# RWKV-5 attention and a multiplicative FFN in one kernel: the general arm's loads and stores move from SyncE's queue to ScalarE's

## The chip, the cores and the metric

The kernel runs on 1 core of one Trainium2 chip. Its time is the device time of one execution in microseconds (us). The time before is the median of three runs; one more execution was recorded by the hardware profiler, and the profile is of that one.

The core has five engines with an instruction stream each: TensorE (PE in the profile; its weight loads are PEld), VectorE (DVE), ScalarE (ACT), GpSimd (POOL) and SyncE (SP). SyncE computes nothing: it issues DMAs and waits on semaphores. ScalarE can issue DMAs too, between its own computations.

## The reference

Two blocks follow each other. The first is a linear attention with a decaying state, for 4 batches, 8 heads, 768 steps and a head size of 48:

```python
def _attn_ref(r, k, v, w, u):
    state = zeros(B, H, D, D)
    for t in range(S):
        cur = einsum('bhd,bhe->bhde', u * k[t], v[t])
        y[t] = einsum('bhd,bhde->bhe', r[t], state + cur)
        state = w * state + einsum('bhd,bhe->bhde', k[t], v[t])
```

The decay `w` is drawn between 0.85 and 0.95, one number per head and channel. The result, as 3072 tokens by 384 features, is `x` of the second block:

```python
def _moe_ref(x, w1, w2, w3, w_out):     # 384x1024, 384x1024, 1024x1024, 1024x384
    a = x @ w1
    b = x @ w2
    return (a * b @ w3) @ w_out
```

The four weight matrices come as 64-bit floats; the kernel turns them into 32-bit floats itself, piece by piece.

## The kernel before

**Tiling.** The 768 steps are cut into 6 chunks of 128; a unit is one chunk of one batch, so there are 24 units. For each unit the kernel loads k, r and v (`load`), scales k and r by powers of the decay, forms the products within the chunk and with the state, and writes a column of `xT`, the transposed input of the second block. For each chunk of 512 tokens (4 batches of 128) it then computes `a`, `b`, their product, and the product with `w34`, which is `w3 @ w_out` computed once. These large products are done with seven half-sized products in place of eight. `store` writes the result, 128 rows at a time. Weights are loaded raw (`fetch`) and turned to 32 bits by integer operations (`magnitude` to `total`).

**Two arms.** The program contains this work twice. First a common part loads `w`, clamps it to between 0.6 and 1.6, and makes a flag that is 1 when no decay was changed by the clamp (lines 294 and 302). All five engines load the flag into a register (line 320) and branch on it (line 1055):

```python
    with tc.If(inside > 0) as chosen:
        program(True)
    with chosen.Else():
        program(False)
```

`program(True)` ends in `listed()`: a hand-written list (`ORDER`) gives the order of every step on every engine, and all of its DMAs are issued from SyncE's queue. `program(False)`, the general arm, ends in `plain()`: it takes any decay, with another way of computing the products within a chunk (`level`), in an order that a scheduler works out. The helpers `load`, `fetch`, `rows_of_u` and `store` are shared by both arms; `fetch` already takes a queue, and the other three issue on `nc.sync`. `W=fetch`, `v`, `kr`, `ub=rows_of_u` and `D=store` are their names in `ORDER`.

**Where the streams lie.** Each engine's stream in the built program holds, one after the other, the common part, the listed arm, a branch at its end (recorded under line 1055, as the branch on the flag is), the general arm, and an end block (recorded under line 1084). In the end block SyncE waits in eight instructions for all semaphores, that of the last store among them, and then all engines meet twice at a barrier. The branch at the end of the listed arm jumps over the general arm to the end block. On SyncE the general arm is 299 instructions of 735 in all, each of 64 bytes.

## Time and profile before

| | |
|---|---|
| three runs | 500.19, 496.93, 497.97 us; median 497.97 us |
| the profiled execution, own time | 498.07 us |
| its span, first to last instruction | 496.3 us |
| granted TensorE clock, mean | 0.988 |
| TensorE matmuls busy | 474.9 us (96%) |
| weight loads busy (beside the matmuls) | 395.7 us (80%) |
| VectorE busy | 329.5 us (66%) |
| ScalarE busy | 198.0 us (40%) |
| GpSimd busy | 65.5 us (13%) |
| SyncE's DMA queue | 51.86 MB, 40.5% of 16 engines |
| instruction queues | 42 packets with 0.69 MB and 24 with 0.20 MB |

The times of the profile are counted from the span's start. "Busy" does not contain waits, branches and DMA issues; SyncE, which has nothing else, has no busy time. The stage views give, for a stretch of time, the busy time of each engine and the number of its instructions. A DMA issue's time "to landing" ends when the last of its semaphore updates is recorded. Instruction queues are DMA queues that bring the engines their own instructions.

### The profile page before, as it was taken

The page shows a single profiled execution, that of the slowest core. Times are in us where ns is not written, and L with a number is a line of the kernel's source. Part 1 is how long each engine was busy: PE and PEld are TensorE (multiplying, and loading weights), DVE is VectorE, ACT ScalarE, POOL GpSimd, SP SyncE. Part 2 cuts the span into 40 slices and gives each one's busy share as a digit, 9 for nine tenths or more (in the row PEclk, how much of TensorE's full clock was granted, in tenths as well). Part 3 has the DMA queues.
Part 4 walks back from the last instruction along what each step waited for, and adds up shares of the span by engine and source line. Part 5 has one row for each costly group of instructions (what it writes and reads, how often), then busy time and mean ns, then how long its engine had stood idle before and what let it go on. Part 6 is the DMA issues. An engine that isn't in the chain of part 4 may idle for free.

```text
span 496.3 us, 12176 instructions
## 1 busy us (share of the span) xinstructions
PE 474.9 (96%) x5070; PEld 395.7 (80%) x5070; DVE 329.5 (66%) x647; ACT 198.0 (40%) x454; POOL 65.5 (13%) x57
## 2 busy tenths in 40 slices
PE   8698899989999999999999999999999999999994
PEld 7586454656769989997888898899998889888893
DVE  5689899999999257658685993677462536415252
ACT  3766455848622114028516462422263231122200
POOL 3148454445400000000000000000000000000000
PEclk9998999999999999999999999999999999999998
DMA  8988968989931004326524550144240000000002
GB/s 187 243 203 240 223 188 227 235 212 242 228 66 45 2 32 114 97 76 166 145 65 112 126 133 17 22 127 126 68 141 1 0 3 33 33 1 0 1 1 71
DMA packets 100482, 52.75 MB, mean 106 GB/s; under 512 B 79296, under 2 KB 89792, under 8 KB 100416
## 3 DMA queue, kind: packets, MB, share of 16 engines
q1 hardware_dynamic: 99792, 51.86, 40.5%
q8 instruction: 42, 0.69, 0.6%
q14 instruction: 24, 0.20, 0.1%
q10 hardware_dynamic: 624, 0.00, 0.1%
HBM read 39.65 MB, written 12.19 MB: 104 GB/s over the span
## 4 chain that ended last, share of the span: by engine, by line
PE 78%; DVE 7%; ACT 4%; DMA 3%; issue 2%; POOL 1%; SPq 1%; ACTq 0%; DVEq 0%; POOLq 0%
PE ps_accB L922 10%; PE ps_w L427 6%; PE ps_Ab L922 4%; PE ps_accC L926 3%; PE ps_accC L922 3%; PE ps_accB L926 3%; PE ps_Aa L922 3%; PE ps_s4b L817 3%; PE ps_a12b L817 3%; PE ps_a11b L817 3%; PE ps_s3t L817 3%; PE ps_s1t L817 3%; PE ps_a22t L817 3%; PE ps_s2t L817 3%; DMA raw<-in_moe_w_dram 3%; PE ps_a L759 2%
## 5 line engine op out<-in xcount | busy, mean ns | idle before, releaser
L396 POOL TENSOR_SCALAR t<-raw 128x512 f32<-128x512 f32 (+2 forms) x30 | 54.3, 1812 | 60.0 <-DMA raw<-in_moe_w_dram 15.1
L922 PE MATMUL ps_accB<-sumw,w 128*128 128x256 f32 x160 | 45.9, 389 | 0.0
L427 PE MATMUL ps_w<-wo,w3T 128*128 128x384 f32 x128 | 42.7, 488 | 0.1
L427 PEld LDWEIGHTS ps_w<-wo,w3T 128*128 128x128 f32 x128 | 24.0, 190 | 15.6 <-issue 0.4
L471 ACT ACTIVATE ynat<-vnat,dg 128x48 f32<-128x48 f32 x144 | 34.4, 324 | 0.7 <-PE ps_x L729 0.6
L922 PEld LDWEIGHTS ps_accB<-sumw,w 128*128 128x128 f32 x160 | 28.9, 190 | 6.0 <-ACT u2a L939 1.1
L735 ACT COPY xT<-ps_x 128x384 f32<-128x384 f32 x24 | 11.5, 480 | 54.1 <-PE ps_x L729 53.9
L527 ACT COPY kT<-tt 128x1024 f32<-128x1024 f32 x19 | 19.8, 1043 | 25.2 <-PE ps_y L690 18.7
L405 ACT ACTIVATE t<-raw 128x512 uint32<-128x512 uint32 (+2 forms) x32 | 22.8, 712 | 14.1 <-DVE wo L401 8.2
L441 DVE TENSOR_TENSOR krs<-krin,pn_in 128x768 f32<-128x768 f32 (+1 forms) x25 | 23.7, 956 | 5.7 <-PE ps_a L563 4.1
L759 PE MATMUL ps_b<-xT,w 128*128 128x512 f32 (+1 forms) x60 | 23.6, 538 | 0.5 <-DVE half L609 0.5
L926 PE MATMUL ps_accC<-xT,w 128*128 128x256 f32 x80 | 23.8, 380 | 0.0
L926 PE MATMUL ps_accB<-xT,w 128*128 128x256 f32 x80 | 23.8, 379 | 0.0
L922 PE MATMUL ps_accC<-xT,sumw 128*128 128x256 f32 x80 | 23.8, 379 | 0.0
L922 PE MATMUL ps_Ab<-xT,w 128*128 128x256 f32 x80 | 22.6, 385 | 0.4 <-ACT ps_accB L937 0.4
L922 PE MATMUL ps_Aa<-xT,w 128*128 128x256 f32 x80 | 22.3, 382 | 0.4 <-ACT ps_accB L937 0.4
L759 PE MATMUL ps_a<-xT,w 128*128 128x512 f32 (+1 forms) x60 | 22.2, 515 | 0.0
L922 PE MATMUL ps_accB<-sumw,sumw 128*128 128x256 f32 x80 | 20.7, 382 | 0.0
L759 PEld LDWEIGHTS ps_b<-xT,w 128*128 128x128 f32 x60 | 11.9, 205 | 9.6 <-issue 7.6
L621 DVE COPY_PREDICATED AT<-later,ps_a 128x512 f32<-128x512 int32 x24 | 17.6, 731 | 1.8 <-PE ps_a L591 1.4
L570 PE MATMUL ps_a<-kT 64*64 64x64 f32 x768 | 17.2, 226 | 1.5 <-ACT kT L527 0.9
L511 DVE STREAM_TRANSPOSE tr<-krs 128x768 f32<-128x768 f32 x19 | 18.4, 969 | 0.2
(187 smaller groups left out, 1087.7 us busy)
## 6 DMA issues: line engine op xcount, KB each, us to landing
raw<-in_moe_w_dram SPq DMA_DIRECT2D x64, 128.0 KB, 3.6
scratch<-tr SPq DMA_DIRECT2D x19, 384.0 KB, 3.4
raw<-in_moe_w_dram SPq DMA_DIRECT2D x8, 768.0 KB, 6.8
tt<-scratch SPq DMA_DIRECT2D x38, 128.0 KB, 2.9
krin<-in_k_dram SPq DMA_DIRECT2D x24, 192.0 KB, 3.9
krin<-in_r_dram SPq DMA_DIRECT2D x24, 192.0 KB, 4.5
vnat<-in_v_dram SPq DMA_DIRECT2D x24, 192.0 KB, 3.5
raw<-in_moe_w_out_dram SPq DMA_DIRECT2D x32, 96.0 KB, 3.0
```

Source lines behind the costliest of these rows:

```text
L396: nc.gpsimd.tensor_scalar(part["t", i].bitcast(F32), words(i)[1].bitcast(F32), 0.0, None, ALU.mult)
L405: nc.scalar.activation(out=part["t", i], in_=words(i)[0], func=COPY, scale=2.0 ** -29)
L427: nc.tensor.matmul(ps, lhsT=w3T[j][:, kc, :], rhs=wo[kc], start=(kc == 0), stop=(kc == KF - 1))
L441: nc.vector.tensor_mul(krs[n % NS][:, which, :, :D], kr[:, which], pn[:, which, :, :D])
L471: nc.scalar.activation(out=ynat[n][:, h, :], in_=vnat[n % NV][:, h, :], func=COPY, scale=dg[n][:, h:h + 1])
L511: nc.vector.transpose(out=blocks[n].rearrange("x m e t -> x e m t"), in_=krs[n % NS][:, :, :, :D])
L527: nc.scalar.copy(out=turned(n).rearrange("x g p (z t) -> x (g p) z t", t=Q), in_=tts.rearrange("x z e t -> x e z t"))
L621: nc.vector.copy_predicated(AT[n], later.bitcast(I32)[:, None, None, :].to_broadcast([C, 2, NP, T]), upper(n))
L759: nc.tensor.matmul(ps, lhsT=(w1 if x == "a" else w2)[:, z, q, js], rhs=xT[c][:, q, ts], start=(q == 0), stop=(q == KM - 1))
L817: nc.tensor.matmul(ps, lhsT=operand(c, j // 2, a)[:, j % 2, m * C:(m + 1) * C], rhs=w34[:, KH * (x == 1) + j, :DH] if x < 2 else made[b][: ...
L922: nc.tensor.matmul(ps, lhsT=quarter(w, g, i, x), rhs=(b11, b21, b22, t4, b12, t2, t3)[x], start=x in (0, 4) and i == 0, stop=True, skip_gr ...
L926: nc.tensor.matmul(ps, lhsT=wide_of[w][:, g + half * HZ, 2, i * P:(i + 1) * P], rhs=xT[c][:, 2, side * TH:(side + 1) * TH], start=False, s ...
```

## The change

`load`, `rows_of_u` and `store` get an argument that names the queue, with SyncE's as its default. In `plain()` each of their calls, and that of `fetch`, hands over ScalarE's. `listed()` and the common part are as they were.

```diff
-    def load(n, which="krv"):
+    def load(n, which="krv", queue=nc.sync):
...
-                nc.sync.dma_start(out=dst, in_=src[b, :, ts, :].rearrange("h t d -> t h d"))
+                queue.dma_start(out=dst, in_=src[b, :, ts, :].rearrange("h t d -> t h d"))
...
-        def rows_of_u():
-            nc.sync.dma_start(out=ub.rearrange("t h d -> t (h d)"),
+        def rows_of_u(queue=nc.sync):
+            queue.dma_start(out=ub.rearrange("t h d -> t (h d)"),
...
-        def store(c, m, x):
+        def store(c, m, x, queue=nc.sync):
...
-            nc.sync.dma_start(out=out[row:row + C, :], in_=made["top" if x else "low", c, m])
+            queue.dma_start(out=out[row:row + C, :], in_=made["top" if x else "low", c, m])
...
-                        store(c, m, x)
+                        store(c, m, x, nc.scalar)
...
-                    fetch(i)
+                    fetch(i, nc.scalar)
...
-                    load(n + 2, "krv")
+                    load(n + 2, "krv", nc.scalar)
...
-            rows_of_u()
-            load(1, "v")
+            rows_of_u(nc.scalar)
+            load(1, "v", nc.scalar)
```

In the built program 195 DMA issues of the general arm pass from SyncE's stream to ScalarE's. SyncE keeps one instruction in that arm, the mark at its end. The scheduler places the general arm's other instructions anew; its streams on VectorE and TensorE become 3 instructions shorter and 1 longer.

## The prediction

> **What bounds the kernel now.** The page comes first. TensorE is busy for 474.9 of 496.3 us, and the chain that ended last is 78% TensorE. The edited functions run in the general arm alone. The inputs' flag (lines 294, 302, 320) selects the listed arm, and the page's costliest TensorE group, L922, is of a function that only this arm calls. So no edited instruction is executed, and a gain or loss can come only from how the program is laid out: from getting past an arm that isn't run. That happens once per engine, at the end of the listed arm, so I read the last microseconds next. First, the branches (asked by line 1055, from 480 us on):

> ```profile
> L1055 PEldq COMPARE_BRANCH  x1: 4014/4014/4014, 485.8 to 485.8; - x1
> L1055 DVEq COMPARE_BRANCH  x1: 57/57/57, 489.0 to 489.0; - x1
> L1055 SPq COMPARE_BRANCH  x1: 43/43/43, 489.7 to 489.7; - x1
> ```

> Each engine leaves the listed arm by one taken branch (TensorE's record has its stall in it). The next instruction of each is in the end block, line 1084. SyncE's, in the windows 489-493 us and 492.9-497 us (op, count, ns, first and last start):

> ```profile
> L1084 SPq EVENT_SEMAPHORE  x3: 17/28/28, 492.6 to 492.8; - x3
> ...
> L1084 SPq EVENT_SEMAPHORE  x7: 17/28/28, 495.1 to 496.2; - x7
> L1084 SPq DRAIN  x3: 7/7/7, 495.5 to 495.8; - x3
> ```

> So SyncE issues its last store at 489.33, ends its branch at 489.77, makes three waits from 492.63, and the fourth (for the last store) starts only at 495.13. After that everything ends within 1.18 us, at 496.30. The table by stage (stretch, its length, busy time of TensorE, weight load, VectorE, ScalarE, GpSimd, then clock, DMA share, GB/s) shows these two holes:

> ```profile
> 489.70:492.70 3.00, 0.00 (x0) 0.00 (x0) 0.00 (x0) 0.00 (x0) 0.00 (x0) 0.78 0.43 142
> 492.70:495.20 2.50, 0.00 (x0) 0.00 (x0) 0.00 (x0) 0.00 (x0) 0.00 (x0) 0.50 0.02 7
> ```

> No engine computes (five times x0). In the first hole the last store is in flight (142 GB/s, issue to landing 2.9 us: the last of its 16 semaphore updates is at 492.19). In the second almost nothing moves. The DMA view of 492.7-495.1 says what does:

> ```profile
> DMA packets 2, 0.02 MB, mean 7 GB/s; under 512 B 0, under 2 KB 0, under 8 KB 0
> q14 instruction: 2, 0.02, 1.6%
> ```

> Two packets of 8,192 bytes on an instruction queue, and no data. So SyncE's stalls look like instruction fetches: 2.86 us after the jump (489.77 to 492.63), then 2.32 us between the third and fourth instruction behind it (492.81 to 495.13). The end of the program hangs on SyncE: the fourth wait's semaphore was complete 2.9 us earlier, and the other engines wait at the barrier (VectorE from 492.45, TensorE from 489.99, ScalarE from 473).

> **The change, part by part.**
> 1. *SyncE's stream shrinks* from 735 to 437 instructions; everything up to the branch is the same byte for byte. The branch is still number 421, but the end block is 424-436: two instructions on, in the page that SyncE is executing since 285 us, and 33 before the next edge. Removed: 2.86 us and 2.32 us.
> 2. *What stands in their place.* The store covers most of the first hole. SyncE may wait for it from about 489.9 on, but it lands at 492.19; SyncE waits that ended on a landing went on 0.02 us after it (at 80.46 and 124.70 us). So its fourth wait passes at 492.21 instead of 495.13. The rest is a fixed tail: from 495.128 to the end, 1.175 us. New end 492.21 + 1.18 = 493.38. **Gain 496.30 - 493.38 = 2.9 us**, not 5.2.
> 3. *What is late next.* SyncE would reach the barrier at 492.21 + 0.44 = 492.65. VectorE, whose jump still misses (489.02 to 492.40), signals at 492.45, 0.2 us before. If the store's last piece landed with its other 15 (491.52), VectorE would set the end and the gain would be 3.1 us; if VectorE's jump were then also as short as ScalarE's (470.7 to 473.1, 2.4 us), SyncE would again be last, at 491.98: 3.6.
> 4. *A short taken branch.* No taken branch inside a loaded page is in this trace; the untaken ones at the If took 0.04-0.09 us. Below: the branch reloads its page all the same, 2.86 us, as the exits of all five engines did. Above: 0.05 us. By nearness of form (a taken branch) the stall is nearer; by cause (no page missing) the untaken one is. I take the latter. It matters little: with the reload SyncE resumes at 492.63, the first hole still ends only 0.4 us after the landing, and the second is gone because the target is mid-page: gain 2.3 us.
> 5. *ScalarE's general arm grows* by 185 instructions with the moved issues; VectorE's is 3 shorter, TensorE's 1 longer, GpSimd's the same. All four still jump out of their loaded pages, as before. ScalarE jumps at 470.7 and waits at 473.1, 22 us ahead of the end; if its price were doubled nothing would show. GpSimd jumps at 134. TensorE waits from 489.99; a second fetch after its jump as long as SyncE's 2.3-2.9 us would end by 492.9 and hold the barrier 0.3 us; the edges that its own instruction packets suggest lie some 60 instructions away.
> 6. *The listed arm* has the same instructions in the same order on each queue. Only where ScalarE and TensorE count up their semaphores differs (377 counting instructions for 373, 803 for 823); each wait is released by the same instruction as before. Every DMA, on SP's, ACT's and POOL's queues, stays in place. I cost it at 0; an update more or less rides on an instruction that runs anyway.
> 7. *Moved issues*: in the general arm 195 issues now stand behind ScalarE's copies and scalings. That arm isn't run here: 0.

> Sum, against the profiled execution's own time of 498.07 (1.77 us outside its span, which I leave as it is): 498.07 - 2.9 = 495.2. The median of the runs, 497.97, less 2.9 gives **495.1**.

> [...] This trace has packets of 8,192 bytes on SyncE's queue, edges 128 apart and two holes of 2.86 and 2.32 us: gain 2.9. [...]

> **The rivals.**
> - *The short jump reloads too* (19%): 495.8 on its own scale less 0.1, 495.7. For: all five exits seen stalled 2.4-4.0 us. Against: all five targets were out of the loaded pages.
> - *The second hole is the store, not a fetch* (10%): the wait in which SyncE stands at 495.13 is the one for the last store; if writes complete later than the landing records say, removing fetches uncovers that wait: 498.0, no change. Against: VectorE, waiting for the store before, went on 0.03 us after its recorded landing (488.19 to 488.22), and the data queue is silent after 492.6.
> [...]
> - *The change does not reach the executed stream*: excluded, since the end block moved from 722 to 424.

> **How the numbers follow.** Free jump 68%, reload 19%, no gain 10%, slower 3%. Forecast 495.1. Mechanism bounds: 494.4 (point 3's 3.6) to 498.0. The three runs before spread over 3.3 us, so a median may lie 1-1.5 us off: the range is 493.6 to 497.3; what is left out is most of the no-gain case and the slower one. Changes under 1% (5 us) are about what a measurement of this kernel can't tell from none: a true 2.9 passes 5 only with some 2 us of luck between two medians, 13%; slower by over 1% 3%; within 84%.

> **What would show it.** Right: SyncE's first line-1084 record within 0.3 us of its branch; its fourth close to 492.2 (2.9 us after the last issue); span 493.4; two fewer q14 packets in the last 8 us. Reload: first record 2-3 us after the branch, then no second hole, span 494.0. Wrong: the fourth wait again about 5.8 us after the last issue, or a difference ahead of 489 us.

## The result, and the profile after

The changed kernel takes 0.9954 of the time of the kernel before (95% interval 0.9934 to 0.9973): its median is 496.61 us over 22 runs (493.36 to 499.40), beside 499.03 us over 22 runs of the kernel before (496.13 to 501.31). That is 2.3 us less (1.3 to 3.3), where 2.9 us was forecast: a small gain, inside the 1% band.

The profiled execution took 498.53 us with a span of 496.7 us, no less than before (498.07 and 496.3). This single pair doesn't show the gain, because its last store was issued later, at 491.22 us instead of 489.33, though the instructions up to there are the same. The difference arises early: TensorE starts its 100th matmul at 12.78 us before and 12.77 after, its 1000th at 70.07 and 72.48. The stage 20-75 us (columns as in the prediction's table by stage), before and then after:

```profile
20.00:75.00 55.00, 47.59 (x695) 32.79 (x694) 47.05 (x74) 32.49 (x65) 29.19 (x18) 0.94 0.84 222
```

```profile
20.00:75.00 55.00, 46.79 (x683) 30.53 (x682) 45.48 (x71) 30.50 (x61) 27.36 (x18) 0.91 0.80 221
```

The granted clock was 0.94 there before and 0.91 after, and 1.00 in both from 75 us to 489. An estimate from these: 0.03 of 55 us, some 1.7 us of the 1.9. So I measure each profile from its last store's issue on SyncE. From there to the end it was 6.97 us before and 5.46 us after.

The views of the changed kernel that answer to those of the kernel before are, first, the branches under line 1055 from 480 us on (count, ns shortest/median/longest, first and last start):

```profile
L1055 PEldq COMPARE_BRANCH  x1: 3874/3874/3874, 487.7 to 487.7; - x1
L1055 DVEq COMPARE_BRANCH  x1: 57/57/57, 490.8 to 490.8; - x1
L1055 SPq COMPARE_BRANCH  x1: 43/43/43, 491.6 to 491.6; - x1
```

Then SyncE's end block, line 1084, in the windows 491-495.3 us and 495.3-497 us:

```profile
L1084 SPq EVENT_SEMAPHORE  x3: 17/28/28, 491.8 to 492.8; - x3
...
L1084 SPq EVENT_SEMAPHORE  x7: 17/28/28, 495.5 to 496.6; - x7
L1084 SPq DRAIN  x3: 7/7/7, 495.9 to 496.2; - x3
```

TensorE still stalls in its branch, 3.9 us. SyncE does not: its first wait starts at 491.8, 0.15 us after the branch ended (2.86 us before). But the fourth wait, the one for the last store, again starts late, at 495.5: 4.33 us after the store's issue, where I had put 2.88. The DMA view of 491-496.7 us shows the reason:

```profile
DMA packets 291, 0.43 MB, mean 75 GB/s; under 512 B 32, under 2 KB 288, under 8 KB 288
## 3 DMA queue, kind: packets, MB, share of 16 engines
q1 hardware_dynamic: 288, 0.39, 20.3%
q8 instruction: 1, 0.02, 2.0%
q14 instruction: 2, 0.02, 1.0%
issues: line engine op xcount, KB each, median us to landing
out_dram<-osb_top SPq DMA_DIRECT2D x1, 192.0 KB, 4.3
```

The last column of the last line is the time from issue to landing. The last store landed after 4.3 us, not after the 2.9 us of the kernel before; 15 of its 16 semaphore updates were there after 2.53 us, one came at 4.31. Beside it run three instruction packets: one of TensorE's (q8; at 1.19 us after the issue, 1.8 us long, so until 2.98) and two on q14 (at 0.93 and 3.36), which fit VectorE's jump.

The trace shows the store standing still behind TensorE's packet. In the DMA view of 493.30-494.18 us (2.08 to 2.96 us after the issue) no packet starts; in that of 494.18-495.10 the store's last nine follow, eight of 1,536 bytes and one of 4:

```profile
DMA packets 0, 0.00 MB, mean 0 GB/s; under 512 B 0, under 2 KB 0, under 8 KB 0
```

```profile
q1 hardware_dynamic: 9, 0.01, 6.3%
```

The first of these starts at 2.97 us, as TensorE's packet ends. (The records name a packet's queue and not its DMA engine; that TensorE's packet and these shared one is inferred from the pause.) In the whole run q14 carried 21 packets of 8,192 bytes where it carried 24 (from the span's start on); in the last 6 us, counted from the last issue, it carried 2 for 4, with one more at 6.45 before.

### The profile page after: what moved, and what is told of

It reads as the page before. It is cut to its first block, busy times and chain, and to the rows that moved or that the text cites. A ratio compares the mean times of both kernels' runs of the same rounds, so it can differ in the third digit from the quotient of the medians.

```text
span 496.7 us, 12176 instructions
## 1 busy us (share of the span) xinstructions
PE 476.6 (96%) x5070; PEld 395.0 (80%) x5070; DVE 328.5 (66%) x647; ACT 197.2 (40%) x454; POOL 62.1 (13%) x57
## 4 chain that ended last, share of the span: by engine, by line
PE 82%; DVE 7%; issue 2%; ACT 2%; POOL 2%; DMA 1%; SPq 1%; ACTq 0%; POOLq 0%; DVEq 0%
PE ps_accB L922 10%; PE ps_w L427 6%; PE ps_Ab L922 4%; PE ps_accC L926 3%; PE ps_accC L922 3%; PE ps_a L759 3%; PE ps_s4b L817 3%; PE ps_accB L926 3%; PE ps_a12b L817 3%; PE ps_Aa L922 3%; PE ps_a11b L817 3%; PE ps_s3t L817 3%; PE ps_s1t L817 3%; PE ps_s2t L817 3%; PE ps_a22t L817 3%; PE ps_b L759 3%
## 5 line engine op out<-in xcount | busy, mean ns | idle before, releaser
L396 POOL TENSOR_SCALAR t<-raw 128x512 f32<-128x512 f32 (+2 forms) x30 | 52.4, 1747 | 64.0 <-PE ps_a L570 9.0
L922 PE MATMUL ps_accB<-sumw,w 128*128 128x256 f32 x160 | 45.9, 389 | 0.0
L922 PEld LDWEIGHTS ps_accB<-sumw,w 128*128 128x128 f32 x160 | 28.9, 190 | 6.0 <-ACT u2a L939 1.1
L759 PE MATMUL ps_a<-xT,w 128*128 128x512 f32 (+1 forms) x60 | 24.4, 555 | 0.8 <-ACT xT L735 0.8
L922 PE MATMUL ps_accC<-xT,sumw 128*128 128x256 f32 x80 | 23.8, 379 | 0.0
L922 PE MATMUL ps_Ab<-xT,w 128*128 128x256 f32 x80 | 22.6, 384 | 0.4 <-ACT ps_accB L937 0.4
L759 PE MATMUL ps_b<-xT,w 128*128 128x512 f32 (+1 forms) x60 | 22.2, 512 | 0.5 <-DVE half L609 0.5
L922 PE MATMUL ps_Aa<-xT,w 128*128 128x256 f32 x80 | 22.3, 381 | 0.4 <-ACT ps_accB L937 0.4
L922 PE MATMUL ps_accB<-sumw,sumw 128*128 128x256 f32 x80 | 20.7, 382 | 0.0
L759 PEld LDWEIGHTS ps_a<-xT,w 128*128 128x128 f32 x60 | 11.9, 204 | 10.7 <-issue 8.8
L713 PE MATMUL ps_y<-vodd,AT 64*64 64x48 f32 x384 | 15.6, 222 | 4.4 <-DVE AT L702 3.4
```

Of the source, the lines that this page charges most:

```text
L396: nc.gpsimd.tensor_scalar(part["t", i].bitcast(F32), words(i)[1].bitcast(F32), 0.0, None, ALU.mult)
L713: nc.tensor.matmul(yt[n][i][rows(a), p, :], lhsT=AT[n][rows(at), i, p, :], rhs=values, start=not (c or a or p), stop=True, skip_group_chec ...
L759: nc.tensor.matmul(ps, lhsT=(w1 if x == "a" else w2)[:, z, q, js], rhs=xT[c][:, q, ts], start=(q == 0), stop=(q == KM - 1))
L922: nc.tensor.matmul(ps, lhsT=quarter(w, g, i, x), rhs=(b11, b21, b22, t4, b12, t2, t3)[x], start=x in (0, 4) and i == 0, stop=True, skip_gr ...
```

## The experiments

The theory to test had two halves. **Placement**: SyncE's two holes were instruction fetches, and where a jump lands among the pages decides them, not its length. **Landing**: with the holes gone the last store sets the end, and the exit fetches of TensorE and VectorE hold up its last piece. All times in this table count from the last store's issue, in us; the ratio is to the kernel before, with its 95% interval.

| kernel | SyncE: branch end to next | fourth wait | last store landed | end | ratio |
|---|---|---|---|---|---|
| before | 2.86 | 5.79 | 2.86 | 6.97 | |
| changed | 0.15 | 4.33 | 4.31 | 5.46 | 0.9954 (0.9934-0.9973) |
| e1_empty | 0.15 | 1.88 | 1.87 | 3.02 | 0.9941 (0.9914-0.9968) |
| e2_stores | 2.77 | 3.39 | 2.78 | 4.52 | 0.9969 (0.9945-0.9993) |
| e3_loads | 0.43 | 4.09 | 4.08 | 5.23 | 0.9986 (0.9959-1.0012) |
| e4_shift3 | 2.77 | 3.44 | 3.01 | 4.57 | 1.0000 (0.9970-1.0030) |
| e4_again | 2.58 | 3.81 | 3.80 | 4.95 | 0.9965 (0.9945-0.9985) |
| e5_pe | 0.15 | 2.07 | 2.05 | 3.21 | |
| e5_dve | 0.15 | 2.68 | 2.67 | 3.82 | |
| e7_both | 0.15 | 3.58 | 3.56 | 4.72 | |
| after_again | 0.15 | 4.32 | 4.30 | 5.45 | 0.9968 (0.9938-0.9998) |
| e8_late7 | 0.15 | 2.22 | 2.21 | 3.36 | 0.9943 (0.9919-0.9966) |
| e6_swap | no jump | 1.86 | 1.84 | 2.99 | 1.0087 (1.0049-1.0124) |

Kernels without a ratio were run once. The kernel before was profiled once, so that its tail of 6.97 us, with which all tails are compared, has no second measurement.

### e4_shift3 and e4_again: the edge moved, the jump kept

```diff
             rows_of_u()
+            rows_of_u()
+            rows_of_u()
+            rows_of_u()
             load(1, "v")
```

> The kernel before, with the load of u's rows written three more times in the general arm, which isn't run: SyncE's end block moves from instruction 722 to 726, so that the page edge at 725 lies ahead of it and not inside. Theory: the jump is longer by 4 instructions, the first hole stays at 2.9 us, the second (2.3 us) is gone: last issue to end 4.6 to 5.5 us instead of 7.0, time 1.5 to 2.3 us below before, ratio 0.9955. Rival 1 (distance or size of the stream): no less than before, 7.0 us. Rival 2 (store): fourth wait again 5.8 us after the last issue, 7.0 us.

This is the kernel before with three more loads in an arm that isn't run; the end block begins at instruction 726. SyncE's branch and end block (lines 1058 and 1087 in this kernel):

```profile
L1058 SPq COMPARE_BRANCH  x1: 43/43/43, 491.7 to 491.7; - x1
...
L1087 SPq EVENT_SEMAPHORE  x10: 17/28/28, 494.5 to 495.8; - x10
L1087 SPq DRAIN  x3: 7/7/7, 495.0 to 495.4; - x3
```

The first hole stands (491.7 to 494.5), and all ten semaphore instructions then follow within 1.3 us: the second hole is gone, though the jump became longer. So the second hole was the page edge inside the end block, and neither the jump's length nor the store. The page edge worked out from SyncE's earlier packets, 725, is confirmed. From last issue to end it was 4.57 us instead of 6.97.

The timed runs didn't show this gain, so I ran it again with more rounds.

> The same kernel as e4_shift3, more rounds. Its profile had the second hole gone and 2.4 us less between last issue and end, its timed runs showed no gain (1.000, 0.997 to 1.003). If the second hole costs an unprofiled execution what it costs a profiled one, the ratio is 0.9952; if it stands in profiled executions alone, the ratio is 1.000 and the changed kernel's gain must come from the first hole.

The second profile again has no second hole; here the landing (3.80 us) sets the fourth wait. The timed ratio was 0.9965 this time. The landing of this one kernel thus differed by 0.8 us between two executions. The two intervals overlap between 0.9970 and 0.9985, short of the 0.9952 that the profile's 2.4 us would give. That the edge costs unprofiled executions something is likely; that it costs them the whole 2.4 us is not shown.

### e2_stores and e3_loads: half of the change each

In e2_stores the edits of the changed kernel on loads, `fetch` and `rows_of_u` are undone:

```diff
-                    fetch(i, nc.scalar)
+                    fetch(i)
...
-                    load(n + 2, "krv", nc.scalar)
+                    load(n + 2, "krv")
...
-            rows_of_u(nc.scalar)
-            load(1, "v", nc.scalar)
+            rows_of_u()
+            load(1, "v")
```

In e3_loads the store's edit is undone:

```diff
-                        store(c, m, x, nc.scalar)
+                        store(c, m, x)
```

> Only the general arm's stores move to ScalarE's queue; its loads stay with SyncE. SyncE's end block then begins 255 instructions behind the branch instead of 301: still outside the two loaded pages, but in mid-page. Theory (page placement decides): the first hole stays at 2.9 us, the second is gone; fourth wait some 3.4 to 4.3 us after the last issue, last issue to end 4.6 to 5.5 us (before 7.0). Rival 1 (the cost grows with the distance of the jump): both holes stay and shrink by a sixth, about 6.2 us. Rival 2 (the second hole is the store completing): fourth wait again 5.8 us after the issue, 7.0 us to the end, no change of time.

> Only the general arm's loads move; its stores stay with SyncE. SyncE's end block begins 51 instructions behind the branch, in the next page, which has been fetched ahead since 285 us. Theory (a jump within the two loaded pages is free): no hole on SyncE, first end-block record within 0.3 us of the branch, last issue to end as with the changed kernel, 4 to 5.5 us. Rival (only the page in execution counts, the branch drops the other): a first hole of 2.9 us and no second, last issue to end 4.6 to 5.5 us.

With the stores alone moved, SyncE jumps 256 instructions (255 was put), past its page and the next one, into a page's middle: first hole 2.77 us, no second. With the loads alone moved it jumps 51, into the page fetched ahead: no hole of 2 to 3 us (0.43 us, somewhat above the 0.3 I had put). So SyncE reached a target in the page in execution in 0.15 us (changed kernel) and one in the next page in 0.43 us, and one past both only after 2.77 us. This settles the rival that any taken branch reloads its page. In these two profiles the first hole was worth nothing: e3_loads, with no hole, ended its tail later than e2_stores, with one (5.23 and 4.52 us), because its store landed at 4.08 instead of 2.78. Its timed ratio, 0.9986, is not clear of 1, though its tail is 1.7 us shorter than before.

### e1_empty: no far jump on any engine

```diff
     with tc.If(inside > 0) as chosen:
         program(True)
-    with chosen.Else():
-        program(False)
```

> The general arm's body is left out (nothing behind the Else), so that every engine's branch at the end of the listed arm jumps a few instructions on. Theory (SyncE's two holes were instruction fetches; with them gone the last store's landing sets the end, and that landing is late because the exit fetches of TensorE and VectorE run beside it): no engine stalls at its exit and no instruction packet starts after 488 us; the last store lands 2.0 to 2.3 us after its issue (kernel before 2.9, changed kernel 4.3); last issue to end about 3.3 us (before 7.0, changed 5.5), so some 3.7 us below the kernel before, ratio 0.9925. Rival 1 (the last store takes its 4.3 us whatever the fetches do): last issue to end again 5.5 us, 1.5 us below before. Rival 2 (no more to be had than from SyncE): like the changed kernel, ratio 0.9955.

Its branches (line 1055), and its DMA view of 490.8-494.2 us:

```profile
L1055 PEldq COMPARE_BRANCH  x1: 193/193/193, 487.6 to 487.6; - x1
L1055 DVEq COMPARE_BRANCH  x1: 57/57/57, 490.7 to 490.7; - x1
L1055 SPq COMPARE_BRANCH  x1: 43/43/43, 491.5 to 491.5; - x1
```

```profile
q1 hardware_dynamic: 288, 0.39, 32.7%
issues: line engine op xcount, KB each, median us to landing
out_dram<-osb_top SPq DMA_DIRECT2D x1, 192.0 KB, 1.9
```

TensorE's branch takes 0.19 us instead of 3.9, no instruction packet is in the view, and the same store, of the same 288 data packets (with the one before it), lands in 1.9 us instead of 4.3. So the landing of 4.3 us does not belong to the store; it comes from the far jumps of the other engines. The end is 3.02 us behind the issue, 2.4 us ahead of the changed kernel. That is about the most the exits can give.

### e5_pe, e5_dve and e7_both: whose far jump delays the store

Here e1_empty gets an Else arm of idle work on TensorE, on VectorE, or on both:

```diff
+    with chosen.Else():
+        with tc.tile_pool(name="psZ", bufs=1, space=PSUM) as psZ:
+            far = psZ.tile([P, C], F32, name="ps_far")
+            for _ in range(1500):
+                nc.tensor.matmul(far, lhsT=ident, rhs=ident, start=True, stop=True)
+            for _ in range(800):
+                nc.vector.memset(warm, 0.0)
```

> The general arm's body is replaced by 1500 matmuls on TensorE (the general arm's own computation is left out), so that only TensorE jumps far at its exit; the other engines jump a few instructions. Theory (the exit fetches delay the last store's landing; TensorE's packets are the long ones, 1.1 to 1.8 us): TensorE stalls 4 us and its page packet starts 1 to 2 us after the last issue, the store lands 3 us or later (1.9 without any fetch, 4.3 in the changed kernel), last issue to end above 4 us. Rival (VectorE's packets do it): landing 1.9 us, last issue to end 3.0 us as in the empty arm.

> The general arm's body is replaced by 800 small memsets on VectorE (the general arm's own computation is left out), so that only VectorE jumps far. Theory (TensorE's packets are the ones that count): VectorE stalls 3 us, the store lands 1.9 to 2.5 us after its issue; the end then hangs on VectorE's arrival at the barrier, 2.9 us after the last issue, last issue to end 3.6 to 3.9 us. Rival (VectorE's packets delay the landing): landing 3 us or later, above 4 us to the end.

My guess at TensorE fell. TensorE alone jumped far, with a 1.2 us packet from 1.72 us on, and the store still landed at 2.05. VectorE alone brought it to 2.67. Neither comes near 4.3, so the next run let both jump.

> The general arm's body is replaced by 1500 matmuls on TensorE and 800 memsets on VectorE (its own computation is left out), so that these two engines jump far and SyncE doesn't. TensorE alone: landing 2.05 us after the issue; VectorE alone: 2.67. Theory (the two delay the landing together, when TensorE's long packet and VectorE's meet the store's packets): landing 2.8 to 4.4 us, last issue to end 4 to 5.5 us, as the changed kernel's 4.31 and 5.46. Rival (the changed kernel's 4.31 has another cause): 2.7 us and 3.8 us, as VectorE alone.

Both together gave 3.56 us, and TensorE's packet now starts earlier after the issue (1.09 us). That is more than either alone, and most of the way from 1.87 to 4.3. In this kernel SyncE, ScalarE and GpSimd don't jump far, so two engines' exits are enough. As in the changed kernel, the store's last packets pause, here until 2.32 us after the issue, when TensorE's packet ends; in e5_pe the store's last packet started at 1.71, as TensorE's began, so that nothing stood behind it. One profile each doesn't say how the rest is shared.

### after_again: is the late landing a matter of luck?

The changed kernel once more, unedited.

> The changed kernel itself, looked at once more beside the others. Ratio 0.9954 (0.9934 to 0.9973) as before. SyncE's end block again begins 0.2 us behind its branch. If the landing of 4.31 us is a matter of how packets fall, it differs here (2.7 to 4.4 us) and last issue to end follows it with 1.15 us more, but not under 3.9 us, VectorE's arrival at the barrier plus 1.1; if it is fixed, 4.3 and 5.5 us again.

Landing 4.30 us, end 5.45 us: as in the first profile, to 0.01 us. That they agree so closely is chance: here TensorE's packet ran from 0.70 to 2.51 us and sixteen packets of 1,536 bytes came behind it, where it ran from 1.19 to 2.98 with eight behind it. Two profiles are few, but the late landing is no single accident of the first one, and its cause was the same both times.

### e8_late7: TensorE sent off later

```diff
-E.5.0.1 E.5.0.5 D.5.0.0 E.5.0.7 D.5.0.1
+E.5.0.1 E.5.0.5 D.5.0.0 E.5.0.7 D.5.0.1 Z.7.1
```

> The changed kernel with 7 idle matmuls of TensorE behind the last product of the listed arm, so that TensorE leaves some 1.5 us later and its third page packet starts about 2.7 us after the last issue instead of 1.2. Theory (that packet and VectorE's together hold up the store's last piece): landing 2.7 us, last issue to end 3.8 us, 1.6 us below the changed kernel, ratio to before 0.992 to 0.995. Rival (TensorE's second packet, now about 1 us before to 0.5 us behind the issue, does as much harm): landing 3.5 us or later, no gain over the changed kernel.

`Z.7.1` calls `busy_array`, seven idle matmuls (14 instructions in the trace) behind TensorE's last product. The DMA view of 490.9-494.4 us, and SyncE's end block:

```profile
q1 hardware_dynamic: 288, 0.39, 32.0%
q8 instruction: 1, 0.02, 1.7%
q14 instruction: 2, 0.02, 1.6%
issues: line engine op xcount, KB each, median us to landing
out_dram<-osb_top SPq DMA_DIRECT2D x1, 192.0 KB, 2.2
```

```profile
L1084 SPq EVENT_SEMAPHORE  x10: 17/28/28, 491.9 to 494.3; - x10
L1084 SPq DRAIN  x3: 7/7/7, 493.5 to 493.8; - x3
```

The same three instruction packets as in the changed kernel, but TensorE's starts at 2.85 us after the issue instead of 1.19, when the store has landed (2.21). End 3.36 us after the issue: 2.1 us less than the changed kernel, and only 0.3 us over the empty arm. There is no pause in the store. So the overlap in time is what held it up. The other profiles agree: in all five that landed at 3.5 us or later (changed, after_again, e3_loads, e4_again, e7_both) the store's last packets resumed within 0.02 us of the end of TensorE's packet, and in the others nothing paused so. The ratio to the kernel before, 0.9943, is the lowest of any kernel that keeps both arms. Its interval overlaps the changed kernel's, so that the step of 2.1 us is shown in the profile's tail and not by the timed runs.

### e6_swap: the far jump at the start

```diff
-    with tc.If(inside > 0) as chosen:
-        program(True)
-    with chosen.Else():
-        program(False)
+    with tc.If(inside < 1) as chosen:
+        program(False)
+    with chosen.Else():
+        program(True)
```

> The changed kernel with its arms in the other order: the condition is turned around, the general arm comes first, the listed arm behind it. Each engine's far jump is then at the branch on the flag, 6 to 9 us after the start, and none at the end but the fall into the end block. Theory: tail as with the empty arm, 3.0 us from the last issue (changed kernel 5.5), and 2.4 to 4 us of stall at the start, of which 2 us or more reach the first products, since VectorE and ScalarE wait there for nothing else: within 1 us of the changed kernel, ratio to before 0.993 to 0.999. Rival (the start is hidden behind the first loads, which are in flight then): 2.4 us below the changed kernel, ratio 0.991.

The tail is what was expected, 2.99 us. The start isn't. Its branches under line 1055:

```profile
L1055 DVEq COMPARE_BRANCH  x1: 67/67/67, 7.7 to 7.7; - x1
L1055 PEldq COMPARE_BRANCH  x1: 5609/5609/5609, 8.1 to 8.1; - x1
```

VectorE's next instruction starts at 13.16 us and ScalarE's at 14.12. The stalls are 5.4 us, 5.6 us (TensorE) and 4.9 us, not the 2.4 to 4.0 of the exits. The stage table (stretch, its length, busy time of TensorE, weight load, VectorE, ScalarE, GpSimd, clock, DMA share, GB/s) of the kernel with swapped arms:

```profile
6.50:14.00 7.50, 2.17 (x17) 1.80 (x15) 1.56 (x7) 1.48 (x3) 0.68 (x2) 0.98 0.99 235
```

and of the kernel before:

```profile
6.50:14.00 7.50, 6.54 (x104) 5.36 (x102) 4.96 (x15) 4.98 (x13) 0.68 (x2) 1.00 1.05 249
```

In these 7.5 us TensorE does 17 matmuls instead of 104, while the DMA engines are full in both (0.99 and 1.05). TensorE's 100th matmul after the start comes 5.9 us later (18.71 and 12.78), and its 1000th 5.8 us later (75.82 and 70.07). This outweighs the end's gain of 4.0 us. The last store is issued 8.6 us later than before; the other 2.8 us come behind the 1000th matmul, and their cause is open.

That the full DMA queues lengthen the fetch is the near reading, but it isn't the whole. GpSimd leaves the listed arm of the kernel before in the midst of the run, from 134.13 to 137.30 us, and the DMA view of 134.2-137.3 us there has the engines as full:

```profile
q1 hardware_dynamic: 1802, 0.65, 100.9%
```

Its stall was 3.2 us (3.2 to 4.8 in the eight profiles in which it jumps far there), less than the 4.9 to 5.6 us of the other three at the start of e6_swap. (There GpSimd's next instruction came 5.4 us behind its branch, but that one waits for a load of v: in the kernel before, without a far jump at that place, it came 5.6 us behind.) At the start four engines jump at about the same time as well (branches at 6.2 to 9.1 us); a start without loads in flight wasn't tried.

## Why the prediction was right or wrong, point by point

**Which view decides: right.** Nothing of the arm that runs was changed, and in the profiles the gain lies behind the last store's issue. The later issue in the profile after, one of the prediction's signs of being wrong, goes with the granted clock (see the result); the instructions up to there are the same.

**Steps 1 and 4, the holes: right.** The first end-block record came 0.15 us behind the branch, within the 0.3 that was put. e4_shift3 confirms the page edge in the end block, e3_loads that the next page was there too. That a taken branch to a loaded page costs next to nothing was my estimate: no trace of the kernel before shows such a branch. The runs showed 0.15 and 0.43 us. The rival with the reload (19%) falls by these runs.

**Step 2, what stands in their place: the mis-sized term.** It kept the store's landing at 2.86 us, as before, and got 2.9 us of gain in the profile. The landing measured 4.31 and 4.30 us, so that the tail became 5.46 us instead of 4.05, and the profiled gain 1.5 us. The timed gain, 2.3 us (1.3 to 3.3), holds both figures, so that its nearness to 2.9 doesn't confirm this step: the two profiles contradict it, and a time so near the forecast is in part luck. The fixed part behind the fourth wait was 1.13 us (1.18 put).

**Step 3, what is late next: half right.** It named the store, and asked only what an earlier landing would give. It had in front of it that the last of the 16 updates came 0.7 us after the other 15, and didn't ask what this one waits on. e1_empty, e7_both and e8_late7 showed that: TensorE's and VectorE's exit packets. Step 5 costed these exits by when their engines reach the barrier, in time; their packets are not harmless. In the kernel before, three packets started at 1.22, 1.54 and 1.78 us after the issue, TensorE's last, when only the store's last few packets were left, and these went on without a pause. In the changed kernel TensorE's starts at 1.19 (0.70 in the second profile), and part of the store stands behind it. That this makes the late landing is shown by the pause in the traces and by e8_late7, which moves the packet the other way. Why it starts earlier is open. Where TensorE left as long before the issue (3.5 to 3.6 us), it started at 1.71 to 1.84 with SyncE's fetch there (before, e2_stores, e4_shift3) and at 1.19 and 1.09 without it but with VectorE's (changed, e7_both); but with neither (e5_pe) it started at 1.72. So that the fetch which went made room for it is not shown.

**The rival "the second hole is the store": wrong for the kernel before** (e4_shift3 and e2_stores had no second hole), **but its place was the right one**: in the changed kernel the fourth wait is the store's. The slower case (3%) and the rival with an edit that reaches nothing found no support: the 1000th matmul started at 72.48 and 69.77 us in the two profiles of the changed kernel, on both sides of the 70.07 before.

**Step 6, same streams: no contradiction.** The last issue came at 489.33 us before, and at 491.22 and 492.32 us in the two profiles of the changed kernel. In the other kernels, e6_swap aside, it spread from 485.01 to 491.28; see the last section.

## What to carry to other kernels

At the end of a program with an arm that isn't run, ask what each engine pays for the jump over it (here 2.4 to 4.0 us) and where the page edges fall: in e4_shift3 an edit in dead code took 2.4 us off the profile's tail. Read the last microseconds from the last store's issue, engine by engine. When a stall goes, what stands behind it sets the end: ask what else is in flight beside that transfer, and don't take over its old landing time. Here the last store's last nine packets started only at 2.97 us, as another engine's instruction packet ended, and it landed at 4.31 us instead of 2.86. Idle work on an engine that nobody waits for can be worth its time, if it moves that engine's traffic out of the way of the last transfer (here 2.1 us in the profile's tail).

## What the runs showed of the hardware that I had not expected

- A store of 192 KB landed in 1.87 us alone, 2.67 us beside VectorE's exit fetch, 3.56 us beside VectorE's and TensorE's, and 4.3 us in the changed kernel. The delay sits in its last update: 15 of 16 were there by 2.61 us in e7_both and by 2.53 us in the changed kernel. In both, the last share of the store waited until TensorE's instruction packet had passed (2.32 us after the issue in e7_both, 2.98 in the changed kernel).
- A far jump out of the listed arm cost 2.4 us (ScalarE) to 4.0 us (TensorE) in the kernel before, GpSimd's 3.2 us amid full DMA engines among them; at the start of e6_swap, where the DMA engines were full too and four engines jumped at about the same time, it cost 4.9 us (ScalarE) to 5.6 us (TensorE).
- The time of the same listed arm goes with the granted TensorE clock, which differs between executions in the first 130 us. Of two executions, e7_both's and after_again's,

```profile
core 0: 489.7 us, clock 1.000
```

```profile
core 0: 497.8 us, clock 0.987
```

the first issued its last store at 485.01 us and the second at 492.32 us. Of these 7.3 us, 6.3 are there at TensorE's 1500th matmul (119.13 and 125.47 us). The granted clock was 1.00 throughout in e7_both up to its last store; in after_again it was 0.94 in 20-75 us, 0.97 in 75-130 us and 1.00 from there to 490. An estimate from these, 0.06 and 0.03 of 55 us each: some 5 us of the 7.3. Whether the clock or the waits of this loading phase come first isn't shown. The 7.3 us are larger than every effect studied here, which is why the tails were compared and not the spans.
